# A limit of two small loads under way on SyncE's queue, in an RWKV-5 layer with a multiplicative FFN

## The chip, the cores and the metric

The kernel runs on one core of one Trainium2 chip. Its time is the device time of one execution, in microseconds (us); lower is better. The engines are named as in the profile: PE (TensorE, the matrix array), DVE (VectorE), ACT (ScalarE), POOL (GpSimd) and SP (SyncE, which here only issues transfers).

## The reference

The first half is a linear attention with decay, over 4 batches, 8 heads, 768 tokens and a head dimension of 48. The second half is an FFN without a nonlinearity, over 3072 tokens, 384 to 1024 features and back. r, k, v, w, u and the output are float32; the FFN's weights are float64, and the kernel gets them as 64-bit words.

```python
for t in range(S):                       # batch, n_heads, seq, head_dim = (4, 8, 768, 48)
    cur = einsum('bhd,bhe->bhde', u[None] * k[t], v[t])
    y[t] = einsum('bhd,bhde->bhe', r[t], state + cur)
    state = w[None, :, :, None] * state + einsum('bhd,bhe->bhde', k[t], v[t])
x = y.transpose(0, 2, 1, 3).reshape(3072, 384)
out = ((x @ w1) * (x @ w2)) @ w3 @ w_out # w1, w2: 384 x 1024; w3: 1024 x 1024; w_out: 1024 x 384
```

## The kernel before

**Tiling.** The tokens are cut into 6 chunks of 128 for each of the 4 batches: 24 units, numbered 0 to 23, batch by batch within a chunk. A unit needs three loads of 192 KB: k and r into one of three `krin` buffers and v into one of three `vnat` buffers. Each is cut by head and token into rows of 192 bytes (`load`, L193 to L200). All three go out from SP (`nc.sync`).

**Weights.** The weights come in pieces through three `raw` buffers (`fetch`, L214 to L219, also on SP): pieces 0 to 7 are strips of w1 and w2 in turn, 768 KB each; 8 to 15 are w_out, 384 KB each; 16 to 31 are w3, 512 KB each. As the words are 64 bits wide, each piece is turned into float32 by five steps: M (ACT), N (DVE), H (DVE), L (ACT) and Q (DVE).

**A unit's steps**, by the letters that the list uses: kk, rr and v are its loads. d, e, f (DVE) make the diagonal term, from k and r and the vector u; g (ACT) or h (DVE) places it. k (DVE) scales k and r by powers of w. T and R (PE) turn k and r, t and r (ACT) take them out. From unit 5 on another way is taken in place of these four: x (DVE) turns 32 x 32 blocks, y (L477) writes them to DRAM, z (L485, four transfers) reads them back in another order, both on SP, and l (ACT, L490) copies k's part. U (PE, L517) forms what the unit adds to the state, A (PE, L524) the products of tokens, m (DVE) masks them. i and j (DVE) update the state, o and p (ACT, L549) spread it. S (PE, L624), V (PE, L638) and Y (ACT, L646) give the unit's output, which is the FFN's input.

**The FFN's steps.** a and b (PE, L664) are the products with w1 and w2 for one block of 128 features, c (ACT) takes the first out of PSUM, u (DVE) multiplies the two. G, K, F, X fold w3 and w_out into one matrix; B, s, P and E form the last product by a scheme of seven block products for eight; D (L754) stores a tile of the output from SP. Two PSUM buffers serve a, b, F and P.

**Order.** Nothing here is scheduled by a planner. The section ahead of the list (L231 to L287) and the list `ORDER` are both inside `tc.manual_schedule`, so each engine runs its instructions in the order in which they are written. SP therefore issues its transfers in the list's order too, and if one must wait, all that is written after it on SP waits. Ahead of the list SP issues, in this order: half of w, k0, r0, W0 (strip 0), v0, u (`ub`), k1, r1, W1, v1. The list goes on with k2, r2, v2, W2, k3, r3, k4, r4, W3, k5, r5, W4, v3, k6, r6, v4, W5, W6, k7, r7, v5, y5, v6, and the four transfers z5. PE begins with 14 products of a constant tile (`keep_busy(14)`). A value computed on the chip from w chooses between the list (`fast`, taken here) and `plain()`, a general path; both are in the program.

```python
for name, *at in (word.split(".") for word in ORDER.split()):
    names[name](*map(int, at))
```

Of the kernel before, what the change touches and what calls it, by code (L numbers as in the profile page):

```python
# [14 lines left out]
COPY = mybir.ActivationFunctionType.Copy  # L15
ABS = mybir.ActivationFunctionType.Abs
PSUM = bass.MemoryType.PSUM
PE, ACT, DVE, SP = (getattr(mybir.EngineType, x) for x in ("PE", "Activation", "DVE", "SP"))


# [72 lines left out]
def kernel(  # L93
# [34 lines left out]
    nc = tc.nc  # L128
# [61 lines left out]
    units = [(c, b) for c in range(NCH) for b in range(B)]  # L190
    NU = len(units)

    def load(n, which="krv"):  # L193
        if n >= NU:
            return
        c, b = units[n]
        ts = slice(c * C, (c + 1) * C)
        for nm, src, dst in (("k", k, krin[n % NIN][:, 0]), ("r", r, krin[n % NIN][:, 1]), ("v", v, vnat[n % NV][:, :, :D])):
            if nm in which:
                nc.sync.dma_start(out=dst, in_=src[b, :, ts, :].rearrange("h t d -> t h d"))  # L200

    w1 = const.tile([P, DF // STRIP, KM, STRIP], F32)
    w2 = const.tile([P, DF // STRIP, KM, STRIP], F32)
# [6 lines left out]
    pieces = [src for src, _ in strips] + [moe_w_out[j * P:(j + 1) * P, None, :] for j in range(KF)] \  # L210
        + [moe_w3[j * P:(j + 1) * P, None, z * PIECE:(z + 1) * PIECE] for j in range(KF) for z in range(NW3)]
    landed = {}
# [17 lines left out]

    with tc.manual_schedule(engines={PE, ACT, DVE, SP}), tc.tile_pool(name="psW", bufs=2, space=PSUM) as psW:  # L231
        nc.vector.memset(wucol, 1.0)
        for i, queue in enumerate((nc.sync, nc.scalar)):
            queue.dma_start(out=wucol[i * PAD:i * PAD + D], in_=w.rearrange("(p i) (d o) -> i d p o", i=2, o=1)[i])
        load(0, "kr")
        fetch(0)
        load(0, "v")
        nc.sync.dma_start(out=ub.rearrange("t h d -> t (h d)"),
                          in_=u.rearrange("h d -> (h d)").rearrange("(o n) -> o n", o=1).to_broadcast([P, DM]))
        load(1, "kr")  # L240
        fetch(1)
        load(1, "v")
# [49 lines left out]
    def program(fast):  # L292
        with ExitStack() as arm:
            body(arm, fast)

    def body(arm, fast):
# [4 lines left out]
        once = fold_pool.enter_context(tc.tile_pool(name="fold", bufs=1))  # L301
        psT = arm.enter_context(tc.tile_pool(name="psT", bufs=2, space=PSUM))
        psA = arm.enter_context(tc.tile_pool(name="psA", bufs=1, space=PSUM))
        psY = arm.enter_context(tc.tile_pool(name="psY", bufs=1, space=PSUM))
        psF = arm.enter_context(tc.tile_pool(name="psF", bufs=2, space=PSUM))

# [539 lines left out]
            seven(NCH - 2)  # L846
            seven(NCH - 1)

        at_start = dict(landed)
        (listed if fast else plain)()  # L850
        landed.clear()
        landed.update(at_start)

# [34 lines left out]
```

## Time and profile before

| | |
|---|---|
| Median of 3 runs | 510.42 us (510.0 to 511.5) |
| The profiled execution | 510.0 us; span from its first to its last instruction 508.3 us |
| Mean granted clock of PE | 0.993 |
| Loads of k, r, v (24 each), issue to landing | 2.7 to 7.5 us, median 4.3 |
| 768 KB strips (8), issue to landing | median 6.1 us |
| Stores of an output tile (24), 192 KB | median 1.9 us |
| Read from HBM, written | 39.65 MB, 12.19 MB |
| Moved by SP's queue | 51.85 MB, 37.5% of the time of 16 DMA engines |

The profile is of one execution. Where a line of it ends in brackets, it tells how long the engine stood idle before that instruction and what ended the idle time. SP's rows show how long an issue took, not how long the transfer took: landing comes later and is read from the completion in the trace. The digits of a row cut the span into 40 slices of 12.7 us and give tenths. "Landing" of a transfer here means that its completion has been signalled.

### The profile page before, as it was taken

Reading aid. Unit: us, or ns where it says so; the run is one execution under the profiler, and the core shown is the slowest. Engines: PE = TensorE matmul, PEld = TensorE weight load, DVE = VectorE, ACT = ScalarE, POOL = GpSimd, SP = SyncE. Lnnn points to the kernel's source line nnn. Section 1 sums busy time; section 2 is a strip of 40 time slices with the busy share of each in tenths; the row PEclk is TensorE's granted clock in tenths of the full one; section 3 lists DMA queues with packets and bytes.
Section 4 is the critical chain, followed back from the end, with each engine's and each line's share of the span. In section 5 each row is a group of like instructions: output and inputs, shape, how many; then the busy total and the mean of one; then the engine's idle time right before and its main releaser. Section 6 shows DMA issues by size and latency. Waiting matters only on the chain.

```text
span 508.3 us, 12255 instructions
## 1 busy us (share of the span) xinstructions
PE 491.7 (97%) x5222; PEld 323.3 (64%) x5222; DVE 277.3 (55%) x587; ACT 183.2 (36%) x456; POOL 6.0 (1%) x23
## 2 busy tenths in 40 slices
PE   4789999999999999999999999999999999999996
PEld 4677645455566766577977486554965744855486
DVE  5999997798196857747326522384422215221442
ACT  3786647576186863303103100341062410001000
POOL 4000000000000000000000000000000000000000
PEclk9899999999999999999999999999999999999999
DMA  7997986768358680304403101230050100000001
GB/s 194 231 256 215 257 212 175 219 204 243 113 129 232 186 212 2 79 0 126 120 22 94 48 15 44 52 112 0 17 157 12 38 1 1 15 15 17 1 18 66
DMA packets 96863, 52.72 MB, mean 104 GB/s; under 512 B 77728, under 2 KB 88224, under 8 KB 96800
## 3 DMA queue, kind: packets, MB, share of 16 engines
q1 hardware_dynamic: 96592, 51.85, 37.5%
q8 instruction: 43, 0.70, 0.6%
q14 instruction: 20, 0.16, 0.1%
q10 hardware_dynamic: 208, 0.00, 0.0%
HBM read 39.65 MB, written 12.19 MB: 102 GB/s over the span
## 4 chain that ended last, share of the span: by engine, by line
PE 88%; DMA 5%; DVE 2%; SPq 2%; ACT 1%; issue 1%; DVEq 0%; ACTq 0%
PE ps_b L664 23%; PE ps_a L664 22%; PE ps_w L392 8%; PE ps_y L638 3%; PE ps_y L624 3%; PE ps_s4b L721 3%; PE ps_a12b L721 3%; PE ps_a11b L721 3%; PE ps_a22t L721 3%; PE ps_s1t L721 3%; PE ps_s3t L721 3%; PE ps_s2t L721 3%; PE ps_a L524 3%; PE ps_a L517 2%; PE ps_w3T L382 2%; DMA krin<-in_r_dram 1%
## 5 line engine op out<-in xcount | busy, mean ns | idle before, releaser
L664 PE MATMUL ps_b<-xT,w 128*128 128x512 f32 (+1 forms) x300 | 131.0, 578 | 0.7 <-ACT a L670 0.7
L664 PE MATMUL ps_a<-xT,w 128*128 128x512 f32 (+1 forms) x300 | 131.6, 581 | 0.0
L664 PEld LDWEIGHTS ps_b<-xT,w 128*128 128x128 f32 x300 | 56.1, 190 | 63.1 <-issue 56.9
L675 DVE TENSOR_TENSOR abt<-ps_b,a 128x512 f32<-128x512 f32 (+1 forms) x50 | 33.4, 667 | 110.5 <-PE ps_b L664 110.5
L664 PEld LDWEIGHTS ps_a<-xT,w 128*128 128x128 f32 x300 | 55.2, 190 | 57.0 <-issue 53.8
L670 ACT COPY a<-ps_a 128x512 f32<-128x512 f32 (+1 forms) x50 | 28.3, 565 | 128.5 <-PE ps_a L664 124.2
L549 ACT COPY wide<-st 64x192 f32<-64x192 f32 x88 | 30.6, 348 | 56.2 <-PE ps_y L624 27.9
L392 PE MATMUL ps_w<-wo,w3T 128*128 128x384 f32 x128 | 42.5, 487 | 0.0
L431 ACT ACTIVATE AT<-same,dg 128x64 f32<-128x64 f32 x160 | 40.4, 335 | 5.7 <-DVE dg L420 3.3
L392 PEld LDWEIGHTS ps_w<-wo,w3T 128*128 128x128 f32 x128 | 23.9, 190 | 15.7 <-issue 0.2
L366 ACT ACTIVATE t<-raw 128x512 uint32<-128x512 uint32 (+2 forms) x32 | 22.5, 711 | 8.2 <-DVE w3n L362 4.6
L404 DVE TENSOR_TENSOR krs<-krin,pn_in 128x768 f32<-128x768 f32 x24 | 22.8, 949 | 0.0
L638 PE MATMUL ps_y<-AT,vnat 64*64 64x64 f32 x1152 | 22.6, 222 | 0.1
L624 PEld LDWEIGHTS ps_y<-tt,wide 128*32 128x32 f32 x1056 | 15.9, 110 | 10.4 <-issue 6.6
L517 PE MATMUL ps_a<-vnat,krs 64*64 64x48 f32 x704 | 16.3, 223 | 5.7 <-DVE krs L404 4.2
L638 PEld LDWEIGHTS ps_y<-AT,vnat 64*64 64x64 f32 x1152 | 19.4, 135 | 3.2 <-issue 1.5
L624 PE MATMUL ps_y<-tt,wide 128*32 128x64 f32 x1056 | 19.7, 221 | 1.5 <-ACT xT L646 1.5
L473 DVE STREAM_TRANSPOSE tr<-krs 128x768 f32<-128x768 f32 x19 | 18.5, 973 | 4.9 <-DMA scratch<-tr 4.8
L552 DVE COPY_PREDICATED AT<-later,ps_a 128x512 f32<-128x512 int32 x24 | 17.4, 727 | 5.4 <-PE ps_a L524 3.3
L517 PEld LDWEIGHTS ps_a<-vnat,krs 64*64 64x64 f32 x704 | 14.0, 138 | 9.6 <-issue 9.2
L490 ACT COPY kT<-tt 128x512 f32<-128x512 f32 x19 | 11.7, 618 | 21.1 <-DMA tt<-scratch 17.8
L540 DVE TENSOR_TENSOR st<-ps_a,st 128x192 f32<-128x192 f32 x40 | 13.9, 347 | 8.6 <-PE ps_a L517 4.9
(108 smaller groups left out, 568.8 us busy)
## 6 DMA issues: line engine op xcount, KB each, us to landing
raw<-in_moe_w_dram SPq DMA_DIRECT2D x16, 512.0 KB, 5.2
scratch<-tr SPq DMA_DIRECT2D x19, 384.0 KB, 3.8
raw<-in_moe_w_dram SPq DMA_DIRECT2D x8, 768.0 KB, 6.1
tt<-scratch SPq DMA_DIRECT2D x38, 128.0 KB, 3.0
krin<-in_k_dram SPq DMA_DIRECT2D x24, 192.0 KB, 4.2
krin<-in_r_dram SPq DMA_DIRECT2D x24, 192.0 KB, 4.6
vnat<-in_v_dram SPq DMA_DIRECT2D x24, 192.0 KB, 4.1
raw<-in_moe_w_out_dram SPq DMA_DIRECT2D x8, 384.0 KB, 4.2
```

The lines of the kernel that those rows point to most:

```text
L366: nc.scalar.activation(out=part["t", i], in_=words(i)[0], func=COPY, scale=2.0 ** -29)
L392: nc.tensor.matmul(ps, lhsT=w3T[j][:, kc, :], rhs=wo[kc], start=(kc == 0), stop=(kc == KF - 1))
L404: nc.vector.tensor_mul(krs[n % NS][:, which, :, :D], kr[:, which], pn[:, which, :, :D])
L431: nc.scalar.activation(out=AT[n][:, i, p, :], in_=same, func=COPY, scale=dg[n][:, h:h + 1])
L517: nc.tensor.matmul(added(n)[rows(i), a, p, :], lhsT=kk[rows(a), 2 * p + i, :], rhs=vnat[n % NV][rows(a), 2 * p + i, 0:D], start=True, stop ...
L549: nc.scalar.copy(out=wide[a][n % 2][rows(i), :, i * D:(i + 1) * D], in_=st[units[n][1]][rows(i)])
L624: nc.tensor.matmul(yt[n][g * Q:(g + 1) * Q, a, q, :], lhsT=wide[a][n % 2][:, p, j * Q:(j + 1) * Q], rhs=rw[:, p, 2 * a:2 * a + 2] if fast ...
L638: nc.tensor.matmul(yt[n][rows(g), a, q, :], lhsT=vv[rows(a), x:x + PAD], rhs=AT[n][rows(a), h % 2, h // 2, :], start=(a, g) not in seen, s ...
L664: nc.tensor.matmul(ps, lhsT=(w1 if x == "a" else w2)[:, z, q, js], rhs=xT[c][:, q, ts], start=(q == 0), stop=(q == KM - 1))
L670: nc.scalar.copy(out=a, in_=ps)
L675: nc.vector.tensor_mul(abt[c, j][:, parts_of_tokens[part]], factor["b", c, j, part], factor["sa", c, j, part])
L721: nc.tensor.matmul(ps, lhsT=of[:, m * C:(m + 1) * C], rhs=w34[:, KH * (x == 1) + j, :DH] if x < 2 else made[b][:, j, :], start=(j == 0), s ...
```

## The change

The kernel keeps a list `small` of the loads of k, r and v. From the third on, each such load gets a dependency on the one two places before it in that list: its issue on SP waits until that load has landed. So of the 72 small loads at most two are under way at a time. Strips and other pieces of weights, u, the trips through DRAM and the stores are not counted and get no new wait of their own. The order of all steps, the buffers, the computing and the 14 products ahead of the list stay as they were. The list `small` is set back between the two paths, as `landed` is.

```diff
+ONE_AFTER_THE_OTHER = mybir.DependencyInfo(mybir.DependencyClass.Sync, mybir.DependencyReason.DATA)
...
+    small = []
+
     def load(n, which="krv"):
+
         if n >= NU:
             return
         c, b = units[n]
         ts = slice(c * C, (c + 1) * C)
         for nm, src, dst in (("k", k, krin[n % NIN][:, 0]), ("r", r, krin[n % NIN][:, 1]), ("v", v, vnat[n % NV][:, :, :D])):
             if nm in which:
-                nc.sync.dma_start(out=dst, in_=src[b, :, ts, :].rearrange("h t d -> t h d"))
+                small.append(nc.sync.dma_start(out=dst, in_=src[b, :, ts, :].rearrange("h t d -> t h d")))
+                if len(small) > 2:
+                    tc.add_manual_dep(small[-1].ins, small[-3].ins.name, ONE_AFTER_THE_OTHER, reason="few small pieces at a time")
...
-        at_start = dict(landed)
+        at_start, small_at_start = dict(landed), list(small)
         (listed if fast else plain)()
+        small[:] = small_at_start
         landed.clear()
```

## The prediction

> **What bounds the kernel now.** I read the page first, then what TensorE (PE) waits for, the table of stretches, and SP's timeline over the first 46 us.
>
> ```profile
> PE 491.7 (97%) x5222; PEld 323.3 (64%) x5222; DVE 277.3 (55%) x587; ACT 183.2 (36%) x456; POOL 6.0 (1%) x23
> ...
> DMA  7997986768358680304403101230050100000001
> ```
>
> PE is busy for 97% of the span, so a stall of PE is paid in full unless a later one shrinks. The DMA digits are highest in the first six slices (76 us). The waits of PE over the whole span:
>
> ```profile
> PE ps_a L517 <- DVE krs L404: 4.2, 1, 4.2
> PE ps_y L624 <- ACT xT L646: 1.5, 1, 1.5
> PE ps_rT L451 <- DVE krs L404: 1.3, 1, 1.3
> PE ps_a L517 <- DMA vnat<-in_v_dram: 1.3, 1, 1.3
> PE ps_b L664 <- ACT a L670: 0.7, 1, 0.7
> ```
>
> By the timeline they begin at 8.35, 23.68, 18.74, 32.59 and 94.20 us. After 33.9 us PE hardly waits: what the front loses, the end loses. Stretches (the last two columns are the DMA engines' share and GB/s):
>
> ```profile
> 12.60:20.00 7.40, 6.14 (x104) 4.97 (x104) 6.73 (x13) 5.65 (x13) 0.00 (x0) 0.66 1.04 263
> 30.00:40.00 10.00, 8.73 (x188) 6.87 (x186) 9.46 (x18) 8.46 (x19) 0.00 (x0) 1.00 1.03 291
> 60.00:80.00 20.00, 20.00 (x262) 10.23 (x260) 19.49 (x38) 9.50 (x23) 0.00 (x0) 1.00 0.79 209
> 110.00:200.00 90.00, 90.00 (x1241) 54.84 (x1239) 62.91 (x124) 54.48 (x138) 0.00 (x0) 1.00 0.62 168
> ```
>
> In the front the DMA engines have no free time. SP issues almost all of it, in order:
>
> ```profile
> 5.01 1.05 SPq L200 DMA_DIRECT2D krin<-in_k_dram  x1
> 6.10 2.78 SPq L200 DMA_DIRECT2D krin<-in_r_dram  x1
> 8.93 1.09 SPq L219 DMA_DIRECT2D raw<-in_moe_w_dram  x1
> 10.07 0.49 SPq L200 DMA_DIRECT2D vnat<-in_v_dram  x1
> 11.23 0.37 SPq L200 DMA_DIRECT2D krin<-in_k_dram  x1
> 11.64 2.68 SPq L200 DMA_DIRECT2D krin<-in_r_dram  x1
> ...
> 17.48 3.64 SPq L200 DMA_DIRECT2D krin<-in_k_dram  x1
> ...
> 30.45 2.24 SPq L200 DMA_DIRECT2D krin<-in_r_dram  x1
> ...
> 38.27 3.13 SPq L200 DMA_DIRECT2D vnat<-in_v_dram  x1
> ```
>
> A free issue takes 0.4 to 0.6 us; the long rows are issues held because the queue is full. They end at 8.88, 14.32, 21.12 and 41.40, each shortly before the weight strip ahead lands (9.01, 14.56, 21.39, 41.65). So the queue itself already stops SP, with about three small pieces behind a strip, and it is never empty: transfers land in the order of their issue, a small one mostly 0.6 to 1.0 us after the one before, a 768 KB strip 2.2 to 3.7 us after.
>
> **What the change does to the queue.** Every load of k, r or v (L200) now waits on SP until the one two places before it has landed, instead of going when there is room. Everything written after it on SP waits too: strips (L219), the trips through DRAM (L477, L485) and stores (L754). No computing is added; POOL's queue is untouched. In the trace's landings, of the 21 loads from v0 to v6 (a number is the unit), 20 were issued before that point, by 0.1 to 5.3 us. Where a strip still stands ahead of the waiting load, the wait costs nothing: v0, k1, v1, k2, k3, r3, k5, r5, v3, k6. The strip's 2.2 to 3.7 us are the cover; without it such a wait costs up to the landing time less the step.
>
> Where only small pieces stand ahead, the queue empties and the waiting load lands one full landing time after its issue. That time for a piece with an empty queue: 2.8 us for the first k (issued at 1.41), 2.7 for the k at 202.57, 2.9 for the k at 56.87. I take 2.8, the first one, since it is the same stage; 2.7 and 2.9 are its near bounds. The far lower bound is the store of an output tile, which has the same 192 KB in longer rows and lands 1.9 us after its issue. All other landings keep their steps. The five places (landing before, then new):
>
> 1. r1 waits for v0 (9.76): issue 9.79, lands 12.59 instead of 11.64, +0.95.
> 2. r2 waits for v1 (15.41 + 0.95 = 16.36): 19.19 instead of 17.12, +2.07; v2 waits for k2 (17.28): 20.11, +2.16.
> 3. k4 waits for k3 (22.79 + 2.16 = 24.95): 27.78 instead of 24.05, +3.73.
> 4. r6 waits for v3 (33.73 + 3.73 = 37.46): 40.29 instead of 35.19, +5.10.
> 5. v5 waits for k7 (42.41 + 5.10 = 47.51): 50.34 instead of 44.71, +5.63. y.5 (L477) stands behind it on SP, and z.5 and W.9, W.8 behind that.
>
> **What of it reaches PE.** I follow the first user of each late landing, by the slack before it:
>
> - d.1 starts at 13.13, r1 now lands at 12.59: nothing. d.2 (DVE, 18.51) must wait for 19.19: +0.7 on k.2 and R.2.
> - M.2 (ACT, 21.42) had 0.03 us to spare behind W2 (21.39, now 23.55). M.2, L.1, p.1, Y.0 (0.92 + 0.92 + 0.71 + 0.48) then end at 26.6, and S.1 on PE starts at 26.7 instead of 25.18: +1.55. d.3 waits for r3 (23.46 + 2.16): +1.87 on DVE.
> - M.3 waits for W3 (28.67 + 3.73), +3.7 on ACT; U.3 on PE waits for v3 (37.46): 37.6 instead of 33.87, +3.73.
> - M.5 (39.62) waits for W5 (39.50 + 5.10): +5.0 on ACT. Y.3 had 0.46 us of idle time ahead of it and a.0.0.1 on PE 0.3 after it: +4.3.
> - l.5 (ACT, 50.34) was waiting for z.5's landing: +5.6. p.4 ends at 51.58 + 5.6, S.4 on PE had 0.87 less a 0.13 start-up to spare: 52.45 becomes 57.3, **+4.9**.
>
> These rows carry the readings:
>
> ```profile
> 28.70 0.93 ACT L354 ACTIVATE w<-raw 128x768 f32<-128x768 f32 x1 [0.76 <-DMA raw<-in_moe_w_dram]
> 33.87 0.68 PE L517 MATMUL ps_a<-vnat,krs 64*64 64x48 f32 x32 [1.27 <-DMA vnat<-in_v_dram]
> 50.34 0.62 ACT L490 COPY kT<-tt 128x512 f32<-128x512 f32 x1 [2.99 <-DMA tt<-scratch]
> ```
>
> Next late would be l.6 (+5.6), but A.6 has 1.15 us of slack behind it: 4.45, under 4.9. From there SP's issues are paced by PE and DVE, and all shifts together. The PE waits at 94.20 and 106.72 (0.7 + 0.5 us) could at most give back 1.2; their strips are issued behind z.9, which PE paces, so I count none. Later waits (r10, r11, r13, r16, r18, r21, r23) hold SP by 1 to 3 us, but the products that follow have 2.5, 12 and more us of slack. One has not: v13 at 159.16 would wait for k15, and z.13 behind it lands 0.7 to 1.4 us later, where A.13 has 0.75 to spare: 0 to 0.65, taken as 0.4.
>
> Sum: 4.9 + 0.4 = 5.3 us. The span of 508.3 becomes 513.6, the profiled execution's 510.0 becomes 515.3; the median of the runs shown lies 0.42 above that execution, so 515.7. With landing times of 2.7 and 2.9 the first term is 4.4 and 5.4; with the 1.9 of a store the five places give +0.05, +0.36, +1.03, +1.50 and +1.55, U.3 is then the last that PE feels (1.0), and 511.8 comes out.
>
> For the landing time the trace has 2.8 us. The Trainium skill, page "DMA: Bandwidth & Descriptors", section "Anatomy of one DMA — SWDGE (gpsimd) path", gives about 2.0 us fixed plus the bytes at 436 GB/s; an estimate from it for 192 KB is 2.45 us, by which the sum would be about 3.5 us and not 5.3. Its "Rules for kernel authors" (issue early, wait late) speak against a wait placed ahead of the issue, which is what this change adds.
>
> **Rivals.**
>
> - *Short gaps (513.5).* A piece lands faster than 2.8 in the emptied queue. Midway to the store's 1.9, at 2.35, S.4 is 2.7 late, and with A.13's 0.4 the sum is 3.1. For: the store. Against: no load of k, r or v in the trace landed in under 2.7 us.
> - *Slower clock (518.3).* The granted clock was 0.5 from 10.85 to 17.68 us, after PE had stood still from 8.35; 32 matmuls of L517 took 1.10 us there and 0.68 later. Gaps of 1.3 and 1.5 us left it at 1.0. My longest new gap is 2.3 us (24.4 to 26.7), nearer to the second. A window of 6.83 us at 0.5 costs at most 6.83 x (1 - 0.68/1.10) = 2.6, where PE sets the pace: 515.7 + 2.6.
> - *Strips pass faster: faster (508.8).* Strips landed 2.92, 3.44, 3.67, 2.80, 2.59 and 2.15 us after the transfer ahead. If two pieces disturb a strip less than three, and W1 to W5 all took 2.15, 4.7 us come back; with the short gaps (3.1) that is -1.6. It decides from 3.1 (short gaps) to 5.3 us of saved steps. Against: a step is counted from the landing of the last piece ahead, so only the pieces behind a strip could disturb it.
> - *No effect (510.4).* The waits are not there, or fall where SP was held anyway. SP was indeed held for some 20 us in the front; but it was let go before the landing awaited, by 1 to 5 us.
>
> **How the numbers follow.** Forecast 0.55 (own range 513.9 to 517.2), short gaps 0.18, slower clock 0.12, strips faster 0.08, no effect 0.07. A change under 0.3% (1.5 us) can't be told from none: faster 0.08, same 0.07, slower 0.85. The range of 511.8 to 518.9 leaves out the last two (0.15) and about 0.05 above.
>
> **What would show it.** The held issues of 2 to 4 us go from SP's rows, and SP's waits name DMAs into krin and vnat. PE's waits before R.2, S.1 and U.3 grow, with a new one before S.4; added up some 5 us more by 60 us. PE has no other idle after that but at A.13. The prediction is wrong if r2 lands before 18.5 (then step 2 fails), if W3 or v3 land less than 2 us later than now, if PE's total wait grows by 5 but a half-clock window is added, or if the later stretch gives back more than 1.2 us.

## The result, and the profile after

| | before | after |
|---|---|---|
| Median, range, runs | 510.44 us (510.0 to 511.5), 4 | 516.76 us (515.01 to 518.07), 4 |
| Profiled execution, its span | 510.0, 508.3 us | 517.27, 515.5 us |
| Mean granted clock of PE | 0.993 | 0.983 |

The ratio is 1.0119, with a 95% interval of 1.0083 to 1.0154: 6.1 us lost (4.2 to 7.9). The forecast was 515.7 us, in a range of 511.8 to 518.9. Six lines were added ahead of the code, so L200 is now L204, L451 is L457, L517 is L523, L624 is L630 and L664 is L670.

From the page of the changed kernel, parts 1 and 2:

```profile
PE 497.2 (96%) x5222; PEld 326.7 (63%) x5222; DVE 277.3 (54%) x587; ACT 182.7 (35%) x456; POOL 6.0 (1%) x23
...
PEclk9679999999999999999999999999999999999999
DMA  7898788668637791302601301220050100000001
```

PE runs the same 5222 matmuls and is busy 5.5 us longer; the clock digits of the second and third slice (6 and 7) say why. What PE waits for (line; in total, times, longest):

```profile
PE ps_a L523 <- DVE krs L410: 4.4, 1, 4.4
PE ps_rT L457 <- DVE krs L410: 3.0, 1, 3.0
...
PE ps_y L630 <- ACT xT L652: 0.7, 1, 0.7
...
PE ps_a L530 <- ACT kT L496: 0.5, 1, 0.5
PE ps_b L670 <- DVE abt L681: 0.5, 1, 0.5
PE ps_a L670 <- DVE abt L681: 0.4, 1, 0.4
PE ps_y L630 <- ACT wide L555: 0.3, 1, 0.3
```

R.2's wait (L457) grew from 1.3 to 3.0 us. The waits of S.1 (1.5) and U.3 (1.3) did not grow: they shrank to 0.7 and 0.2. The stretches tell where that time went (PE busy first, then PEld, DVE, ACT, POOL; the last three columns are granted clock, share of the DMA engines, GB/s):

```profile
12.60:20.00 7.40, 6.25 (x104) 5.11 (x104) 5.45 (x10) 5.78 (x13) 0.00 (x0) 0.63 0.81 204
20.00:30.00 10.00, 7.30 (x180) 6.23 (x184) 9.28 (x16) 5.36 (x13) 0.00 (x0) 0.57 0.87 214
30.00:40.00 10.00, 9.82 (x223) 8.27 (x215) 7.31 (x15) 7.78 (x17) 0.00 (x0) 0.92 0.93 224
110.00:200.00 90.00, 88.70 (x1264) 53.62 (x1263) 62.61 (x118) 58.52 (x144) 0.00 (x0) 1.00 0.68 183
```

From 12.6 to 20 us the DMA share fell from 1.04 to 0.81, and from 30 to 40 us from 1.03 to 0.93: the queue runs dry. And PE's clock was halved a second time, so its matmuls filled time that it would else have spent waiting. SP's timeline shows the cause (start, duration of the issue):

```profile
10.00 0.37 SPq L204 DMA_DIRECT2D krin<-in_r_dram  x1
...
16.68 0.37 SPq L204 DMA_DIRECT2D krin<-in_r_dram  x1
17.22 0.45 SPq L204 DMA_DIRECT2D vnat<-in_v_dram  x1
...
24.69 0.37 SPq L204 DMA_DIRECT2D krin<-in_k_dram  x1
25.22 0.46 SPq L204 DMA_DIRECT2D krin<-in_r_dram  x1
...
36.91 0.37 SPq L204 DMA_DIRECT2D krin<-in_r_dram  x1
...
47.58 0.37 SPq L204 DMA_DIRECT2D vnat<-in_v_dram  x1
48.00 0.57 SPq L483 DMA_DIRECT2D scratch<-tr  x1
```

These are r1, r2, v2, k4, r4, r6, v5 and y.5. Up to 50 us an issue of a small load now takes 0.4 to 0.7 us (but for k1 with 0.91 and v6 with 1.83), where some had been held for 2 to 4; it starts late instead: r2 at 16.68, where it had begun at 11.64. The view of SP's waits gives the new releasers, over the whole span:

```profile
SPq L204 <- DMA vnat<-in_v_dram: 30.5, 13, 4.8
...
SPq L204 <- DMA krin<-in_k_dram: 15.5, 9, 5.0
...
SPq L204 <- DMA krin<-in_r_dram: 3.6, 6, 1.0
```

How late each milestone of PE is, profile against profile, in us:

| start on PE | before, at | after | forecast |
|---|---|---|---|
| U.0 | 12.6 | +0.1 | 0 |
| R.2 | 20.1 | +1.9 | +0.7 |
| S.1 | 25.2 | +3.0 | +1.55 |
| U.3 | 33.9 | +3.2 | +3.73 |
| a.0.0.1 | 41.8 | +3.3 | +4.3 |
| S.4 | 52.5 | +4.3 | +4.9 |
| A.8 | 100.2 | +5.8 | +4.9 |
| A.13 | 167.0 | +7.2 | +5.3 |
| end | 508.3 | +7.3 | +5.3 |

### The profile page after: what moved, and what is told of

The parts are those of the page before. It is cut to its first block, busy times and chain, and to the rows that moved or that the text cites. A ratio compares the mean times of both kernels' runs of the same rounds, so it can differ in the third digit from the quotient of the medians.

```text
span 515.5 us, 12256 instructions
## 1 busy us (share of the span) xinstructions
PE 497.2 (96%) x5222; PEld 326.7 (63%) x5222; DVE 277.3 (54%) x587; ACT 182.7 (35%) x456; POOL 6.0 (1%) x23
## 4 chain that ended last, share of the span: by engine, by line
PE 74%; DMA 13%; DVE 6%; ACT 3%; issue 2%; SPq 2%; ACTq 0%; DVEq 0%
PE ps_b L670 19%; PE ps_a L670 17%; PE ps_w L398 6%; DMA raw<-in_moe_w_dram 5%; PE ps_s4b L727 3%; PE ps_a12b L727 3%; PE ps_a11b L727 3%; PE ps_a22t L727 3%; PE ps_s2t L727 3%; PE ps_s1t L727 3%; PE ps_s3t L727 3%; PE ps_y L644 3%; PE ps_y L630 2%; DMA krin<-in_k_dram 2%; PE ps_a L530 2%
## 5 line engine op out<-in xcount | busy, mean ns | idle before, releaser
L670 PE MATMUL ps_b<-xT,w 128*128 128x512 f32 (+1 forms) x300 | 131.2, 579 | 1.1 <-ACT a L676 0.6
L670 PE MATMUL ps_a<-xT,w 128*128 128x512 f32 (+1 forms) x300 | 131.7, 581 | 0.6 <-DVE abt L681 0.4
L670 PEld LDWEIGHTS ps_b<-xT,w 128*128 128x128 f32 x300 | 55.9, 190 | 64.3 <-issue 56.7
L670 PEld LDWEIGHTS ps_a<-xT,w 128*128 128x128 f32 x300 | 55.2, 190 | 58.0 <-issue 53.1
L555 ACT COPY wide<-st 64x192 f32<-64x192 f32 x88 | 30.6, 348 | 57.3 <-PE ps_y L630 28.0
L630 PEld LDWEIGHTS ps_y<-tt,wide 128*32 128x32 f32 x1056 | 16.4, 111 | 10.3 <-issue 6.0
L630 PE MATMUL ps_y<-tt,wide 128*32 128x64 f32 x1056 | 20.6, 224 | 1.0 <-ACT xT L652 0.7
L523 PE MATMUL ps_a<-vnat,krs 64*64 64x48 f32 x704 | 16.7, 227 | 4.7 <-DVE krs L410 4.4
L523 PEld LDWEIGHTS ps_a<-vnat,krs 64*64 64x64 f32 x704 | 14.3, 142 | 8.8 <-issue 7.8
L530 PEld LDWEIGHTS ps_a<-tt,kT 64*64 64x64 f32 x768 | 15.1, 145 | 7.4 <-issue 2.8
```

Source lines behind the costliest of these rows:

```text
L523: nc.tensor.matmul(added(n)[rows(i), a, p, :], lhsT=kk[rows(a), 2 * p + i, :], rhs=vnat[n % NV][rows(a), 2 * p + i, 0:D], start=True, stop ...
L530: nc.tensor.matmul(upper(n)[rows(a), i, p, :], lhsT=kT[n][rows(i), p, rows(a)], rhs=rT[n][rows(i), p, 2 * a:2 * a + 2], start=True, stop=True)
L555: nc.scalar.copy(out=wide[a][n % 2][rows(i), :, i * D:(i + 1) * D], in_=st[units[n][1]][rows(i)])
L630: nc.tensor.matmul(yt[n][g * Q:(g + 1) * Q, a, q, :], lhsT=wide[a][n % 2][:, p, j * Q:(j + 1) * Q], rhs=rw[:, p, 2 * a:2 * a + 2] if fast ...
L670: nc.tensor.matmul(ps, lhsT=(w1 if x == "a" else w2)[:, z, q, js], rhs=xT[c][:, q, ts], start=(q == 0), stop=(q == KM - 1))
```

## The experiments

Theory A, the prediction's: SP's wait costs only where the queue runs empty behind it, at five places before 50 us. Against it: that the loss comes evenly from all 70 waits (B), and that PE's slower clock is the loss (C). Each difference in us below is the ratio less one, times the median of before in the same comparison.

**Only the waits at empty places.** Of the 70, the eight on r1, r2, v2, k4, r4, r6, v4 and v5 are kept.

```diff
-                if len(small) > 2:
+                if len(small) - 1 in (4, 7, 8, 11, 12, 17, 18, 21):
```

> Only eight of the new waits are kept, those with nothing but small pieces ahead: on r1, r2, v2, k4, r4, r6, v4 and v5. Theory A (the queue runs empty there): the whole loss of the change, 5 to 6.5 us over the kernel before, 515.5 to 517.0. Rival B (each of the 70 waits costs a little on SP): 8 of 70, under 1 us, 510.5 to 511.3.

517.17 us (514.34 to 518.29), ratio 1.0120 (1.0073 to 1.0166): 6.1 us (3.7 to 8.5). Eight of the 70 waits cost as much as all 70. S.4 is 4.6 us late, the end 6.3.

**Only the others.** The same list, excluded.

```diff
-                if len(small) > 2:
+                if len(small) > 2 and len(small) - 1 not in (4, 7, 8, 11, 12, 17, 18, 21):
```

> The other 62 waits alone, those with a strip ahead and all after v6. Theory A: nothing in the front, 0 to 0.65 us from z.13 late, so 510.4 to 511.2. Rival B: most of the loss, 515 to 516.5.

511.44 us (510.48 to 515.83), ratio 1.0024 (1.0000 to 1.0048): 1.2 us (0 to 2.5), far from the 4 us and more of theory B. If a small loss remains, part of it is at steps that the prediction had cost at nothing. The waits of PE in the profiled execution, at 512.76 us above the median of its 10 runs (S.4 is 1.1 us late in it):

```profile
PE ps_y L644 <- issue: 1.9, 2, 1.3
...
PE ps_b L670 <- ACT a L676: 1.2, 1, 1.2
...
PE ps_a L530 <- ACT kT L496: 0.5, 1, 0.5
```

The wait of 1.2 us in the second line begins at 137.14 us: a `b` waits for `c`, the copy out of PSUM on ScalarE. ScalarE's timeline shows `c` behind l.11, which stands waiting for z.11, and SP issued z.11 late: r14, written ahead of it, went out at 128.21 us instead of 124.63, as it now waits for v11 (the first line is taken up below, with the clock):

```profile
137.19 0.62 ACT L496 COPY kT<-tt 128x512 f32<-128x512 f32 x1 [4.59 <-DMA tt<-scratch]
137.72 0.58 ACT L676 COPY a<-ps_a 128x512 f32<-128x512 f32 x1
```

The prediction had compared such waits with the product that uses the late data, and not with what stands behind l.11 on ScalarE. Its list has r11 and r13, which don't wait, where the trace has r14.

**Only the late waits.** From the 24th load on, 49 of them. (By the order of the list the 24th is k8, and not v7 as the expectation says.)

```diff
-                if len(small) > 2:
+                if len(small) > 23:
```

> The waits start only at the 24th load, v7; the front is issued as before, 48 loads wait. My theory (the front makes the loss, the late waits little): S.4 on PE where it was before (within 0.3 us); later the step of ScalarE behind r11's load and A.13 cost 0.5 to 2.5 us, as they did where only the other waits were left: 510.9 to 512.9 us. Rival (the waits of the whole length share the loss evenly): 48 of 70 waits, so two thirds of 6.3 us, 514 to 515 us.

513.28 us (510.92 to 515.85), ratio 1.0041 (1.0021 to 1.0061): 2.1 us (1.1 to 3.1), below two thirds of the loss. S.4 was 0.8 us late where 0.3 had been expected as the most. No wait of this edit acts before k8 goes out at 50.68 us, and y.5 had already landed 0.5 us late by then, so this is mostly what two executions with the same front differ by; a difference between milestones of less than that decides nothing. The profiled execution, at 511.13 us near the lower end of its 12 runs, shows a wait of 0.72 us at A.13 and one of 0.63 at 243.15, and ends 1.1 us late; the rest of the typical 2.1 isn't located. The costs of the parts are measured no better than to 1 or 2 us, and whether they add up to the whole can't be told.

**A depth of three.**

```diff
-                if len(small) > 2:
-                    tc.add_manual_dep(small[-1].ins, small[-3].ins.name, ONE_AFTER_THE_OTHER, reason="few small pieces at a time")
+                if len(small) > 3:
+                    tc.add_manual_dep(small[-1].ins, small[-4].ins.name, ONE_AFTER_THE_OTHER, reason="few small pieces at a time")
```

> Three small loads under way instead of two. Theory A: the queue held SP at about three pieces already, so the waits nearly coincide with the holding; worked out as before with a landing time of 2.8 us the sum is +0.9 at the trip z.5, with 3.7 us (what the pairs took in the changed kernel) +3.4; half of it is covered by then: 511 to 513. Rival B: as many waits as with two less one, 515 to 516.5.

511.04 us (507.43 to 513.07), ratio 0.9995 (0.9965 to 1.0025): no difference that can be told (-1.8 to +1.3 us), with 69 waits in place. So a wait as such costs nothing that can be measured here, and theory B falls by this too. The trace isn't that of before, though: z.5 landed 3.3 us late, as expected with 3.7 us for a landing, and in the profiled execution, at 511.28 us, S.4 is 1.8 us late and the end 1.3. So three is near the depth to which the full queue holds SP by itself, and not exactly it.

**A depth of one.**

```diff
-                if len(small) > 2:
-                    tc.add_manual_dep(small[-1].ins, small[-3].ins.name, ONE_AFTER_THE_OTHER, reason="few small pieces at a time")
+                if len(small) > 1:
+                    tc.add_manual_dep(small[-1].ins, small[-2].ins.name, ONE_AFTER_THE_OTHER, reason="few small pieces at a time")
```

> One small load under way at a time: every load waits for the one ahead of it. Theory A: nearly each of the 23 loads of the front is now alone behind its strip or behind nothing; worked out as before with 2.8 us the lateness at z.5 is 28 us, with 3.7 us 42 us; strips passing faster take some of it back: 535 to 550. Rival B (a price for each wait, as with two): 516 to 518.

563.46 us (562.49 to 565.12), ratio 1.105 (1.0988 to 1.1112): above the expectation. A piece alone in the queue lands fast, as the page's list of transfers shows (KB, median us from issue to landing; v often has a strip ahead):

```profile
krin<-in_k_dram SPq DMA_DIRECT2D x24, 192.0 KB, 2.6
krin<-in_r_dram SPq DMA_DIRECT2D x24, 192.0 KB, 2.6
vnat<-in_v_dram SPq DMA_DIRECT2D x24, 192.0 KB, 3.6
```

In the changed kernel the same list has 3.8, 3.7 and 4.0. By z.5 this run was 29.5 us late, where the method of the prediction, with 2.8 us for a landing, gives 28. The miss lies behind that: A.8 is 36.9 us late and A.13 51.5, so here the waits of units 8 to 15 cost as well.

**r2 and v2 alone.**

```diff
-                if len(small) > 2:
+                if len(small) - 1 in (7, 8):
```

> Only two waits, on r2 and v2. Theory A: r2 lands 1.1 (landing time 2.8) to 2.0 us (3.7) late, the stream behind it stays late by 1.1 to 1.7, and so does PE from S.1 on: 511.5 to 512.5. If later slack takes it back: 510.4 to 511.

512.25 us (509.3 to 513.64), ratio 1.0032 (1.0005 to 1.0059): 1.6 us. One of the five places is worth about a quarter of the loss, as expected; the profile has U.3 and S.4 2.5 us late.

**The clock, first try.** Matmuls of a constant tile (`Z`, 8 and 6) are put ahead of R.2 and S.1, to keep PE busy.

```diff
-W.3 Q.0 p.0 A.0 M.1 h.1 j.0 S.0 t.1 d.2 R.1 k.2 m.0 r.1 R.2 kk.5 rr.5 e.2 U.1 N.1 r.2 f.2 A.1 M.2 H.1 T.2 i.1 L.1 m.1
-V.0 d.3 p.1 W.4 Q.1 v.3 Y.0 t.2 j.1 S.1 g.2 N.2 A.2 k.3 V.1 H.2 R.3 kk.6 rr.6 Y.1 U.2 m.2 M.3 v.4 T.3 N.3 L.2 a.0.0.0
+W.3 Q.0 p.0 A.0 M.1 h.1 j.0 S.0 t.1 d.2 R.1 k.2 m.0 r.1 Z.8 R.2 kk.5 rr.5 e.2 U.1 N.1 r.2 f.2 A.1 M.2 H.1 T.2 i.1 L.1 m.1
+V.0 d.3 p.1 W.4 Q.1 v.3 Y.0 t.2 j.1 Z.6 S.1 g.2 N.2 A.2 k.3 V.1 H.2 R.3 kk.6 rr.6 Y.1 U.2 m.2 M.3 v.4 T.3 N.3 L.2 a.0.0.0
```

> The changed kernel with 8 dummy products of PE ahead of R.2 and 6 ahead of S.1, where PE stood still or would, so that the granted clock stays at 1.0 after the first half-clock window (mean clock 0.992 or 0.993 instead of 0.983 to 0.988). Theory A (the transfers set the pace): the time stays within 1 us of the changed kernel, 515.5 to 517.5, and PE's waits grow by what its busy time loses. Rival C (the second half-clock window of 10.2 us is the loss): 5 us less, 511 to 512.

521.44 us (520.72 to 522.77), ratio 1.0216 (1.0184 to 1.0248): slower than either side expected. Its waits of PE show something new, stalls without a releaser:

```profile
PE ps_a L530 <- issue: 2.9, 2, 2.2
PE ps_a L670 <- issue: 1.5, 1, 1.5
...
PE ps_a L523 <- issue: 0.8, 1, 0.8
PE ps_y L644 <- issue: 0.8, 1, 0.8
```

With 14 more products in PE's stream (28 matmuls and 28 weight loads in the trace) PE stood for 2.20 us at 46.60, 1.54 at 71.55 and three times some 0.75 later, some 6 us in all, waiting for nothing that the profile shows. Such stalls don't need the added products: the run with the 62 other waits has two, of 0.60 us at 21.96 and 1.27 at 26.76. The traces point to PE's instruction code. In all twelve there are nine stalls of this kind of over 0.25 us, and eight of them ended 1.33 to 1.68 us after the end of a 16 KB packet of instruction code (the changed kernel has 43). No run tested it. The run can't speak on the time, but U.3 started at 37.15 us, against 37.03, with a clock of 1.00 from 20 to 30 us.

**The clock, with the number of matmuls kept.** Six of the 14 products at the start are moved ahead of R.2.

```diff
-W.3 Q.0 p.0 A.0 M.1 h.1 j.0 S.0 t.1 d.2 R.1 k.2 m.0 r.1 R.2 kk.5 rr.5 e.2 U.1 N.1 r.2 f.2 A.1 M.2 H.1 T.2 i.1 L.1 m.1
+W.3 Q.0 p.0 A.0 M.1 h.1 j.0 S.0 t.1 d.2 R.1 k.2 m.0 r.1 Z.6 R.2 kk.5 rr.5 e.2 U.1 N.1 r.2 f.2 A.1 M.2 H.1 T.2 i.1 L.1 m.1
...
-        keep_busy(14)
+        keep_busy(8)
```

> The changed kernel with six of the 14 dummy products moved from the start to just before R.2, where PE stood still for 3.03 us; PE has as many instructions as before, so that its later code lies as it did (the kernel with 14 products more lost time in waits of PE that nothing released). The half-clock window that began at 21.4 us should go or start later. Theory A (transfers set the pace): 515.5 to 517.5, U.3 at 37.0 to 37.3 us as in the changed kernel. Rival C (the clock is the loss): 511 to 512.

516.88 us (515.84 to 522.89, four runs), ratio 1.018 (1.0094 to 1.0265; one run of 522.89 widens it). Stretches and PE's waits:

```profile
12.60:20.00 7.40, 6.29 (x84) 5.28 (x84) 4.69 (x10) 4.82 (x9) 0.00 (x0) 1.00 0.71 144
20.00:30.00 10.00, 7.06 (x228) 6.03 (x228) 8.92 (x16) 6.49 (x16) 0.00 (x0) 0.83 0.89 244
30.00:40.00 10.00, 8.52 (x179) 7.08 (x182) 9.14 (x16) 7.86 (x16) 0.00 (x0) 1.00 0.85 193
```

```profile
PE ps_rT L457 <- DVE krs L410: 2.2, 1, 2.2
PE ps_y L630 <- ACT xT L652: 1.9, 1, 1.9
PE ps_a L523 <- DMA vnat<-in_v_dram: 1.5, 1, 1.5
PE ps_a L670 <- DVE abt L681: 1.2, 1, 1.2
```

The clock is whole but for one window of 3.41 us, and the waits that had vanished before S.1 and U.3 are back (1.9 and 1.5 us). S.1 is 1.0 us late instead of 3.0, and U.3 2.4 instead of 3.2; but S.4 is late by the same 4.3, since y.5 landed at 52.59, against 52.57. The front also begins 1.2 us earlier here (U.0 at 11.43), as it does in the run on x.6 below, which leaves the start as it is, so this isn't the clock alone. It shows that a PE that is faster and earlier in the middle gains nothing at S.4. Nor does the time go with the clock from run to run: 516.15 us at a mean of 0.997, 515.84 at 0.986, 517.61 at 0.985, 522.89 at 0.993. Theory C falls: the second half-clock window is there, and took the place of waiting.

**A strip moved ahead.** W2 and W3 are written in front of r2 and of k4, to stand ahead of the loads that found the queue empty.

```diff
-kk.2 rr.2 v.2 d.0 W.2 N.0 e.0 f.0 M.0 k.0 g.0 H.0 U.0 kk.3 rr.3 d.1 T.0 k.1 L.0 R.0 e.1 kk.4 rr.4 t.0 i.0 f.1 r.0 T.1
-W.3 Q.0 p.0 A.0 M.1 h.1 j.0 S.0 t.1 d.2 R.1 k.2 m.0 r.1 R.2 kk.5 rr.5 e.2 U.1 N.1 r.2 f.2 A.1 M.2 H.1 T.2 i.1 L.1 m.1
+kk.2 W.2 rr.2 v.2 d.0 N.0 e.0 f.0 M.0 k.0 g.0 H.0 U.0 kk.3 rr.3 d.1 T.0 k.1 L.0 R.0 e.1 W.3 kk.4 rr.4 t.0 i.0 f.1 r.0 T.1
+Q.0 p.0 A.0 M.1 h.1 j.0 S.0 t.1 d.2 R.1 k.2 m.0 r.1 R.2 kk.5 rr.5 e.2 U.1 N.1 r.2 f.2 A.1 M.2 H.1 T.2 i.1 L.1 m.1
```

> The changed kernel with all its waits, and two strips written earlier on SP: W2 between k2 and r2, W3 ahead of k4. Each then stands ahead of a load that waits, where the queue had run empty. Theory A: r2 and v2 land about as late as in the changed kernel (20.3, 20.9), but W2 lands near 19.5 instead of 23.73 and W3 near 27.5 instead of 31.47; of the 5.9 us of lateness at z.5 some 2.5 to 3 go: 513.5 to 515. Rival B (every wait costs by itself): as the changed kernel, 516 to 517.5.

516.1 us (515.32 to 519.93), ratio 1.0145 (1.0074 to 1.0216): a miss, nothing is seen to be won; S.4 starts at 56.60 us, against 56.71. W2 landed at 20.94 instead of 23.73, but r2 behind it at 21.43 instead of 20.34. SP's timeline (k5, r5, W4, v3):

```profile
29.01 0.37 SPq L204 DMA_DIRECT2D krin<-in_k_dram  x1
30.19 0.37 SPq L204 DMA_DIRECT2D krin<-in_r_dram  x1
30.61 0.57 SPq L225 DMA_DIRECT2D raw<-in_moe_w_dram  x1
31.64 1.12 SPq L204 DMA_DIRECT2D vnat<-in_v_dram  x1
```

W3 landed at 27.85 instead of 31.47, but it had been the cover of k5 and r5. Now these found the queue empty: r5 landed at 34.05 instead of 33.29, W4 at 36.31 instead of 36.20, v3 at 36.97 instead of 36.90. The empty place moved with the strip.

**What PE loses behind S.4.** In the changed kernel PE's waits of 0.4 us at 53.53 and 0.5 at 71.13 are for `u` on VectorE. VectorE's timeline shows x.6 ahead of it:

```profile
52.59 0.98 DVE L479 STREAM_TRANSPOSE tr<-krs 128x768 f32<-128x768 f32 x1 [2.50 <-DMA scratch<-tr]
53.50 0.38 DVE L681 TENSOR_TENSOR abt<-ps_b,a 128x256 f32<-128x256 f32 x1
```

`tr` has one buffer, so x.6 waits until y.5 has landed. Before the change x.6 started at 46.32, 0.65 us after y.5's landing. In the experiment x.6 is written behind this `u`.

```diff
-v.6 A.4 Q.2 g.4 a.0.0.1 k.6 N.5 b.0.0.1 M.6 N.6 m.4 c.0.0.1 H.6 a.0.1.1 z.5 u.0.0.1 L.6 H.5 b.0.1.1 c.0.1.1 x.6 W.9
-L.5 a.0.2.2 u.0.1.1 y.6 i.4 W.8 l.5 Q.6 p.4 d.5 a.0.3.2 Q.5 c.0.2.2 kk.8 rr.8 j.4 N.4 e.5 S.4 H.4 c.0.3.2 M.8 z.6 U.5
+v.6 A.4 Q.2 g.4 a.0.0.1 k.6 N.5 b.0.0.1 M.6 N.6 m.4 c.0.0.1 H.6 a.0.1.1 z.5 u.0.0.1 L.6 H.5 b.0.1.1 c.0.1.1 W.9
+L.5 a.0.2.2 u.0.1.1 x.6 y.6 i.4 W.8 l.5 Q.6 p.4 d.5 a.0.3.2 Q.5 c.0.2.2 kk.8 rr.8 j.4 N.4 e.5 S.4 H.4 c.0.3.2 M.8 z.6 U.5
```

> The changed kernel with one step of VectorE, x.6, written behind u.0.1.1, so that the products already waiting for u are not behind the wait for y.5's landing. My theory (what PE loses after S.4 comes from VectorE standing at x.6 for y.5): PE's wait of 0.40 us at 53.5 us goes, A.8 is 4.8 to 5.4 us late against before in place of 5.8, and the time is 515.5 to 516.5 us. Rival (VectorE is full there either way, or x.6 is then late for z.6): A.8 late by 5.8 or more, and the time 516.5 us or more.

519.22 us (515.41 to 520.63), ratio 1.0166 (1.0143 to 1.0189), an interval that overlaps that of the changed kernel. The profiled execution took 515.41 us, the least of the six. In it the wait at 53.5 is gone, and S.4 starts 3.6 us late instead of 4.3, A.8 5.2 instead of 5.8. But y.5, which the edit doesn't touch, had landed 0.7 us earlier here (51.88 against 52.57), and that is all that S.4 gained. Of what was to be won between S.4 and A.8 nothing is seen: 1.6 us are lost there, against 1.5, with a wait of 0.83 at 99.23 in place of one of 0.56. The time sides with the rival. x.6 made that one wait of 0.4 us; that it costs time in the end isn't shown.

## Why the prediction was right, and where its steps were not

**The mechanism and the place held.** With the eight waits alone the loss is as large as with all; they stand at the five places that the prediction named, and what it called covered cost 1.2 us (0 to 2.5) together with the late waits. The held issues vanished from SP's rows and the waits name k, r and v, as foretold. That the full queue had held SP at about three loads behind a strip fits the depth of three, whose time can't be told from before. "In the front the DMA engines have no free time" said too much: their share was 1.04 and 1.03 in the stretches shown, but 0.92 from 20 to 30 us and 0.75 from 40 to 50.

**Landing by landing** (us from the span's start):

| transfer | before | forecast | after |
|---|---|---|---|
| r1 | 11.64 | 12.59 | 12.73 |
| r2 | 17.12 | 19.19 | 20.34 |
| W2 | 21.39 | 23.55 | 23.73 |
| k4 | 24.05 | 27.78 | 28.38 |
| W3 | 28.67 | 32.40 | 31.47 |
| v3 | 33.73 | 37.46 | 36.90 |
| r6 | 35.19 | 40.29 | 41.12 |
| W5 | 39.50 | 44.60 | 43.72 |
| k7 | 42.41 | 47.51 | 47.52 |
| v5 | 44.71 | 50.34 | 51.61 |
| y.5 | 45.67 | 51.30 | 52.57 |

k7 came out 0.01 us from its forecast, by luck: two terms were wrong in opposite directions, and in other traces in which the same eight loads wait it landed at 46.80 to 48.81.

- *"I take 2.8" for a landing in an empty queue.* That held for r1 alone (2.74). r2, k4, r6 and v5 took 3.66, 3.69, 4.20 and 4.03: 0.9 to 1.4 us more. The pieces that follow within 1.2 us are not the reason, since W1 follows r1 after 0.41 us, and k4 with the same followers took 2.63 and 2.51 in two other runs. What tells the landings apart in the traces is instruction code, which the DMA engines also carry (queue, packets, MB and share, from the page of the changed kernel):

```profile
q8 instruction: 43, 0.70, 0.6%
```

Five traces have all five places (the changed kernel, the eight waits alone, both runs on the clock, x.6), so 25 such landings. In 17 a 16 KB packet of that queue began 0.4 to 2.2 us after the issue; they took 3.03 to 4.76 us and landed 1.32 to 1.66 us after its end. The other 8, where none began or it began by 0.06 us after the issue at the latest, took 2.51 to 2.83. At depth one, of 39 loads that were alone in the queue, the 32 without a packet begun 0.3 to 2.0 us after the issue took 2.50 to 3.34, half of them under 2.6, and six of the other 7 took 3.01 to 4.14. So the 2.8 was right for a landing that no such packet met, and four of the five met one. No run moved the packets, so that they cause it is strongly suggested and not proven. The Trainium skill's estimate of 2.45 us (page "DMA: Bandwidth & Descriptors", section "Anatomy of one DMA — SWDGE (gpsimd) path"), by which the sum would have been 3.5, is made for the gpsimd path and not for SP's; the 2.50 to 3.34 of a lone load lie above it, and the landings that set the pace here far above.
- *"All other landings keep their steps."* The strips' steps shrank: W2 landed 2.82 us after the piece ahead instead of 3.44, W3 2.51 instead of 3.67, W5 1.92 instead of 2.59. That fits a strip that already moves while the last part of the small piece is on its way, though no run separated the two. So the rival "strips pass faster" did occur, to the amount of 2.5 us, and the longer landings outweighed it: y.5 is 1.27 us later than forecast.

**PE.** "d.2 must wait for 19.19: +0.7" was +1.9, by r2's later landing. PE then stood for 3.03 us before R.2, where +0.7 would have made 2.0 and the prediction's longest new gap was to be 2.3, before S.1; and the clock was granted at one half from 21.43 to 31.68 us. The timeline shows the same shapes slow after R.2 and fast later (1.09 and 0.65 us for four matmuls of L457):

```profile
22.00 1.09 PE L457 MATMUL ps_rT<-ident,krs 128*128 128x128 f32 x4 [3.03 <-DVE krs L410]
...
32.70 0.65 PE L457 MATMUL ps_kT<-ident,krs 128*128 128x128 f32 x4
...
37.03 0.68 PE L523 MATMUL ps_a<-vnat,krs 64*64 64x48 f32 x32 [0.18 <-DMA vnat<-in_v_dram]
```

So S.1 was 3.0 late and not 1.55 (1.0 in the run with six products moved, whose clock was better but whose front also began 1.2 us earlier), and the sign "PE's waits grow, some 5 us more by 60 us" failed: they grew by little, and busy time stood in their place. U.3 came at 37.03 for 37.6, a.0.0.1 +3.3 for +4.3, both by the shorter strip steps. The rival "slower clock" was thus right that a window would come and wrong that it would add 2.6 us to the end: it lay where transfers set the pace.

**S.4.** l.5 started at 56.61 (forecast 50.34 + 5.6 = 55.94), and p.4 behind it ended where the prediction put S.4: S.4's first half ran at 56.71, its second waited for p.4 until 57.53, against 57.3. The term of 4.9 measured 4.3 at the first matmul; the chain named for it was the right one.

**"From there all shifts together" failed.** By A.8 another 1.5 us were gone. About 0.7 of it is more waiting (1.42 us of idle time between S.4 and A.8, 0.69 before), the rest lies inside PE's busy rows and was not assigned. The step overlooked is x.6's single buffer on VectorE; it explains 0.4 us of waiting.

**The late waits.** A.13's 0 to 0.65, taken as 0.4, measured 0.53 as a wait of PE. The list of the others was misread from the trace: before the change the late loads that go out over 1 us ahead of the landing two places before them are r10, r14, r15, r16 (4.8 us), r17, v14, r18, r19, r22 and r23, and the load at 159.16 is v14, behind k17. "Slack of 2.5, 12 and more" was reckoned for the unit's products alone; in the run without the eight waits ScalarE, working in order, passed r14's wait on to a `c`, which the profiles of the changed kernel and of the late waits alone don't show. The late waits alone cost 2.1 us (1.1 to 3.1) and not 0.4; with 13 more in the front it was 1.2 (0 to 2.5).

The sum of 5.3 us thus met 6.1 (4.2 to 7.9): the front about right from two errors that happen to cancel, the part behind it too small.

## What to carry to other kernels

A queue that is full paces its issuer at no cost, because work already stands behind the transfer that lands; a wait for an earlier landing, put ahead of the issue, costs nothing while a large transfer is still ahead of it, and a landing time less one step wherever only small ones are. To price such a wait, list what is in the queue at each waiting issue, and allow for the instruction code that the DMA engines carry too: here such a landing took 2.5 to 2.8 us without a packet of it and 3.0 to 4.8 with one. Then follow every engine's in-order successors of the late data, not only its first user: here a buffer's reuse on VectorE and an unrelated copy on ScalarE stood waiting.

## What was not expected of the hardware

- The same 192 KB load in rows of 192 bytes landed 2.59 us after its issue when alone in the queue (median of the 32 lone loads named above), and 3.03 to 4.76 at the empty places where a 16 KB packet of instruction code began meanwhile. In the changed kernel the packets of r2 and v2 ran from 17.5 us; most were done by 19.75, with a thin tail behind (some 20 packets in a quarter of a us, where there had been 300), and a packet of instruction code (1.38 us) had begun at 17.38. The thin tail fits a single late engine; that it is the one with the instruction code is argued, since the trace doesn't name the engines. The Trainium skill says, on the page "DMA: Bandwidth & Descriptors", section "Why a DMA increments its semaphore by 16 and not by 1", that up to 16 engines finish independently and the semaphore counts them all; no run here isolates it.
- A gap of 3.03 us on PE was followed by half clock for 10.24 us; after a gap of 2.15 us in the run with six products moved the clock stayed whole, until a window of 3.41 us at 26.58, after another gap of 1.90. With a depth of three a gap of 2.29 us, ending at 25.17, was followed by a window of 3.41 us as well.
- Fourteen more products in PE's stream came with stalls of up to 2.20 us that have no releaser in the profile, some 6 us in all. Each of these five ended 1.33 to 1.68 us after a 16 KB packet of instruction code; that this is the cause isn't shown.
